# Sliding-window attention and MLP on one core: the transpose of x ahead of the turns by DMA, and k turned one block after q

## The chip, the core and the metric

The kernel runs on one core of one Trainium2 chip. The metric is the device time of one execution in microseconds. The engines are named as the profile names them: PE (TensorE, matmuls), DVE (VectorE), ACT (ScalarE), POOL (GpSimd), SP (SyncE, which here only issues DMAs). PEld is the load of weights into PE.

## The reference

For 8 batches, 8 heads, 576 positions and a head size of 64, attention with a window of 128 keys and a linear bias by distance, and then an MLP with a residual on the joined heads:

```python
scores = scale * np.matmul(q, k.transpose(0, 1, 3, 2))
bias = slopes[:, None, None] * (-np.abs(rel).astype(np.float32))[None, :, :]
mask = (rel >= 0) & (rel < window)
scores = np.where(mask, scores + bias[None], -1000000000.0)
attn = softmax(scores)                      # over the keys
x = (attn @ v), heads joined                # 8 x 576 x 512
xn = (x - mu) / np.sqrt(var + 1e-06) * g_ln
out = x + np.maximum(xn @ w_ch1, 0.0) @ w_ch2    # 512 -> 2048 -> 512
```

## The kernel before

**Blocks.** Two batches form a pair p (0 to 3). Each pair has nine blocks: blocks 0 to 7 are 128 positions of one of the two batches (block `2 i + b` is stretch i of batch b), and block 8, called T, holds the last 64 positions of both. In all there are 36 blocks, numbered n = 9 p + blk. The q and k of two neighbouring blocks (a pair of blocks, index i) are loaded, turned and kept together; the two halves of such a tile are transposed by separate instructions.

**Attention of a block.** `scores` (line 459, matmuls at L436) multiplies the turned q and k into PSUM, with the keys of the block itself and of the block two before it (the same batch, 128 positions back). For block T its call uses the keys of blocks 6 and 7 alone; T's own keys are used by `scores_tail` one block later. ACT takes the exponential (L445), DVE multiplies by the decay of the distance (`masks`, L456), `values` multiplies by v on PE (L489), and DVE divides by the sum (L497, L498) to give x.

**Normalisation.** `stats` takes mean and variance on DVE (L586, L587) and the inverse root on POOL (L541, L544, tile `rstd`). `normal` (line 524) centres and scales on DVE (L528, tile `xc`) and has SP transpose the result by DMA (L536) into `xT`, the MLP's input. Blocks 0 to 7 go another way, with a transpose on PE.

**MLP.** The blocks are gathered in groups: six of two blocks and then six of four (groups 0 to 5 and 6 to 11). `mlp1(g)` is 16 units of matmuls (L735) on all of a group's xT, so it can start when the last block of its group has been transposed. `mlp2` (L768) is the second product for the groups of two. Groups of four use `fast_mlp2` (L834), which multiplies with sums of quarters of w2 and of the hidden layer. The eight DVE instructions that build the sums of w2 (`combine_w2`, L189) are spread over earlier layers.

**q and k.** From pair (1, 2) on, that is from block 13, q and k are loaded by POOL's queue (L234) in a layout that a DMA can transpose, and SP transposes them into the turned tiles (L322, in `turn`): two transposes for q and two for k, one of each for block T. Before that, PE transposes them.

**Order.** The order is written out by hand. `steps` is a list of steps for the attention; for each block n from 8 on it holds

- values(n) and then the scores of block n + 2,
- masks(n + 1), masks(n + 2), stats(n) and the loads up to block n + 8 (`load_until`, on POOL),
- `turn_at(n + 1)`, which turns q and k of a pair that begins at block n + 5 where DMA does it,
- `normal(n)`, with xT(n).

Block 11 is `HURRIED`: normal(10) is put off to stand behind values(11) and the scores of block 13, so that blocks 10 and 11 follow each other with little MLP work between them. `weave_at` mixes the steps with the units of the MLP, unit by unit, by lists of places; `also` lists the units after which one instruction of the sums of w2 is put. Each engine runs its instructions in this order, and SP and POOL issue their DMAs in it. A store waits in SP's queue until its rows have been finished.

Of the kernel before, what the change touches and what calls it, by code (L numbers as in the profile page):

```python
# [22 lines left out]
T = 8  # L23
# [36 lines left out]
def kernel(  # L60
# [10 lines left out]
    nc = tc.nc  # L71
# [136 lines left out]
    raw = {}  # L208

    def by_dma(p, i):  # L210
        return (p, i) >= BY_DMA_TURN
# [41 lines left out]
    order = [(p, blk) for p in range(NPAIR) for blk in range(NSLOT)]  # L253
# [1 line left out]
    weights = {3: w1s + w2s[:2], 5: w2s[2:]}  # L255
    loads, place = [], []
    for n, (p, blk) in enumerate(order):
        if blk % 2 == 0:
            for src, tag in ((q, "q"), (k, "k")):
                loads.append((load_qk, src, tag, p, blk // 2))  # L260
        loads.append((load_v, p, blk))
        place.append(len(loads))
        loads += weights.get(n, [])
# [12 lines left out]
    turned = {}  # L276
# [30 lines left out]
    def turn(p, i, in_sc=False, copies=(nc.vector.tensor_copy, nc.scalar.copy)):  # L307

        k = keys_tile("k", p, i)
        q = queries(p, i) if i < 4 else keys_tile("q", p, i)
        if by_dma(p, i):
            for tag, dst in (("q", q), ("k", k)):
                src = raw.pop((tag, p, i))
                for b in range(2 if i < 4 else 1):
                    t = dst[:, b]
                    if tag == "q" and i < 4:  # L320
                        t = turned["q", p, i][:, b].rearrange("p h r c -> p h (r c)")
                    nc.sync.dma_start_transpose(  # L322
                        out=t, in_=src[:, b].rearrange("p h d -> p (h d)")
                    )
            return
        ps = [bank(b if in_sc else None) for b in range(2)]
        if i < 4:
            transposed("q", p, i, [t[:, 0] for t in ps])
            if p == 0 and i == 1:
                warm(3)  # L330
            transposed("k", p, i, [t[:, 1] for t in ps])
            for b, copy in enumerate(copies):
                copy(out=q[:, b], in_=ps[b][:, 0])
                copy(out=k[:, b].rearrange("p h (c r) -> p r h c", r=2), in_=ps[b][:, 1])
        else:
            for tag, t, dst, copy in zip("qk", ps, (q, k), copies):
                transposed(tag, p, i, [t[:, 0]])
                copy(out=dst[:, 0].rearrange("p h (c r) -> p r h c", r=2), in_=t[:, 0])

    def bank(sc=None):  # L340
        if sc is None:
# [6 lines left out]
    def queries(p, i):  # L348
        if by_dma(p, i):
            t = turned_pool.tile([P, 2, HP, 2, HALF], FP16, tag="q", name="q")  # L350
            turned["q", p, i] = t
            return t
        t = turned_pool.tile([P, 2, 2, HP, HALF], FP16, tag="q", name="q")
        turned["q", p, i] = t.rearrange("p b r h c -> p b h r c")
        return t

    def keys_tile(tag, p, i):
        t = turned_pool.tile([P, 2, HP, P], FP16, tag=tag, name=tag)
        turned[tag, p, i] = t
        return t  # L360
# [259 lines left out]
    for g, size in enumerate(GROUPS):  # L620
        n = sum(GROUPS[:g])
# [3 lines left out]
    count = len(order)  # L625

    def turn_step(n, *how):
        p, blk = order[n]
        return [(turn, p, blk // 2) + how]
# [28 lines left out]
    steps = warm_step(11) + [[(turn_first,)]] + warm_step(3)  # L658
# [7 lines left out]
    first = len(steps)  # L666
# [16 lines left out]
    steps += [[(scores_tail, 0)] + scores_step(9) + masks_of(8)]  # L683


    def turn_at(n):
        ahead = [m for m in (n + 3, n + 4) if m < count and order[m][1] % 2 == 0]
        return [
            f
            for m in ahead  # L690
            if by_dma(order[m][0], order[m][1] // 2) == (m == n + 4)
            for f in turn_step(m, True)
        ]

    steps.append(turn_at(8))
    for n in range(8, count):
        first_half, second_half = values_steps(n)
        step = first_half + second_half[:1]
        if n + 1 < count and order[n + 1][1] == T:
            step += [(scores_tail, order[n][0])]  # L700
        if n + 2 < count:
            step += scores_step(n + 2)
        steps.append(step)
        to_mask = [m for t in (n + 1, n + 2) if t < count for m in masks_of(t)]
        stats_step = [(stats, n)] + load_step(n)
        turns = [turn_at(n + 1)] if n + 1 < count else []
        if n == HURRIED:
            steps += [[(normal, n - 1)], to_mask + stats_step, [(normal, n)], *turns]
        else:
            steps += [to_mask + stats_step, *turns]  # L710
            if n != HURRIED - 1:
                steps.append([(normal, n)])
    combined = combine_w2()
    done = 0

# [10 lines left out]
    def mlp1(g, on_dve=()):  # L726
        xT = turned_x[g]
        w = w1 if g < FIRST_GROUPS else w1g
        cols = len(members[g]) * P
        ht = hidden[g] = hidden_pool.tile([P, NFB, 4 * P], FP16, tag="ht", name="ht")  # L730
        turn_about = chain(*zip(range(QF), range(QF, NFB)))
        for u, fb in enumerate(turn_about if g >= FAST else range(NFB)):
            ps = psum("ps_m1")
            for kb in range(NKB):
                nc.tensor.matmul(  # L735
                    ps[:, 0:cols],
                    w[:, kb, fb * P : (fb + 1) * P],
                    xT[:, kb, 0:cols],
                    start=(kb == 0),
                    stop=(kb == NKB - 1),  # L740
                )
            if u in on_dve:
                nc.vector.tensor_scalar(
                    out=ht[:, fb, 0:cols],
                    in0=ps[:, 0:cols],
                    scalar1=0.0,
                    scalar2=None,
                    op0=ALU.max,
                )
            else:  # L750
                nc.scalar.activation(  # L751
                    out=ht[:, fb, 0:cols], in_=ps[:, 0:cols], func=AF.Relu
                )
            yield cols
            if g >= FAST and u == 10:
                for i in range(4):
                    combine_hidden(g, 0, i)

    def mlp2(g, parts=((0, NFB),)):

        ht = hidden[g]
        sums = {}
        for first, end in parts:
            for at, (p, blk) in enumerate(members[g]):
                if first == 0:
                    sums[at] = ps_mm.tile([P, DM], FP32, tag="mm", name="ps_m2")
                for fb in range(first, end):
                    nc.tensor.matmul(  # L768
                        sums[at],
                        ht[:, fb, at * P : (at + 1) * P],  # L770
                        w2[:, fb, :],
                        start=(fb == 0),
                        stop=(fb == NFB - 1),
                    )
                    if fb % 4 == 3 and fb < NFB - 1:
                        yield DM
                if end == NFB:
                    finish(p, blk, sums[at])
                    yield DM
# [155 lines left out]
    def weave_at(units, *places, also=()):  # L935
        for u, _ in enumerate(units):
            advance_to(done + places.count(u))
            if u in also:
                next(combined, None)
# [13 lines left out]
    with tc.manual_schedule(engines={engine.PE, engine.SP, engine.Pool}):  # L953
        with tc.manual_schedule(engines={engine.Activation, engine.DVE}):
            advance_to(first)
            weave_at(mlp1(0, (0, 1)), 2, 7, 8, 9, 13)
            weave_at(mlp1(1), 2, 8, 12)
            weave_at(mlp2(0, ((0, 8), (8, 12), (12, NFB))), 0, 1, 3, 4, 4, 5)
            weave_at(mlp2(1), 0, 1, 2, 3, 4, 6, 6)
            weave_at(mlp1(2), 0, 3, 3, 6, 8, 11)  # L960
            weave_at(mlp2(2), 0, 2, 4, 6, 7)


            weave_at(mlp1(3, (9, 10, 11)), 8, 8, 12, 15)
            weave_at(mlp2(3), 0, 1, 1, 3, 4, 4, 6, 6)
            weave_at(mlp1(4), 0, 4, 8, 10, 10, 14)
            weave_at(mlp2(4), 0, 2, 2, 5, 5, 7, also=(1, 4, 6))
            weave_at(mlp1(5), 0, 5, 5, 8, 10, 12, also=(3, 6, 9))
            weave_at(mlp2(5), 0, 1, 2, 4, 6, 7)
            ring += [ps_mm.tile([P, DM], FP32, tag="mm", name="ps_r") for _ in range(4)]  # L970
            for g in range(6, len(GROUPS)):
                weave_at(
                    mlp1(g), 0, 2, 5, 7, 8, 10, 13, 15, also=(1, 4) if g == 6 else ()
                )
                weave_at(fast_mlp2(g), 1, 3, 6, 7, 7, 10, 12, 13)
# [31 lines left out]
```

## Time and profile before

| | |
|---|---|
| median of three runs | 315.26 us (314.24 to 315.96) |
| profiled execution | 315.53 us, span 313.8 us |
| mean granted clock of TensorE | 0.987 |
| PE busy | 300.4 us, 96% of the span |
| DVE busy | 220.6 us, 70% |
| ACT busy | 171.7 us, 55% |
| POOL busy | 140.0 us, 45% |
| transposes on SP | xT 28, q 23, k 23; median to landing 4.9, 5.8 and 5.0 us |

The profile is of one execution. Times in it are in us from the start of its span. A row of a timeline has its start, its length, the engine and line, the operation with its output and input, how many instructions were merged, and in brackets the idle time before it with what ended it. "SPq" is SP's issue of a DMA: its length is the time of the issue, and the landing comes later. A share of busy time says little by itself; what matters is which wait ends last where PE stands still.

### The profile page before, as it was taken

How to read it: one execution, taken by the hardware profiler on the slowest of the kernel's cores; microseconds unless marked ns; L12 is line 12 of the kernel's file. 1: busy time of each engine (PE TensorE's matmuls, PEld its weight loads, DVE VectorE, ACT ScalarE, POOL GpSimd, SP SyncE). 2: the span in 40 equal slices, each digit the busy share in tenths (PEclk: the TensorE clock that was granted, in tenths of full speed). 3: DMA queues.
4: the chain of work that ended last, by engine and by line, in shares of the span. 5: the costliest groups of instructions: out<-in, count | busy, mean ns of one | idle time of the engine just before them, and what ended most of it. 6: DMA issues, size and time to landing. Idle time of an engine off the chain costs nothing.

```text
span 313.8 us, 9068 instructions
## 1 busy us (share of the span) xinstructions
PE 300.4 (96%) x3747; PEld 200.8 (64%) x3747; DVE 220.6 (70%) x533; ACT 171.7 (55%) x297; POOL 140.0 (45%) x210
## 2 busy tenths in 40 slices
PE   8989999999999999699999999999999999999994
PEld 2468655757758575334885588558755874685484
DVE  2788877878585787806895799569948995761363
ACT  6587764767658376138427833772487247405600
POOL 8923756781287847822494618553301001100001
PEclk9999999999999999969999999999999999999999
DMA  9999999999799999990999999999945043015004
GB/s 112 164 204 200 185 155 162 198 108 141 94 96 156 159 170 170 145 204 18 105 120 188 144 87 99 174 177 97 138 95 118 19 88 85 18 28 125 0 2 134
DMA packets 150843, 38.28 MB, mean 122 GB/s; under 512 B 141809, under 2 KB 146417, under 8 KB 150802
## 3 DMA queue, kind: packets, MB, share of 16 engines
q0 software_dynamic: 103808, 18.49, 83.6%
q1 hardware_dynamic: 46594, 18.76, 35.7%
q8 instruction: 29, 0.48, 0.7%
q10 hardware_dynamic: 400, 0.46, 0.5%
q14 instruction: 12, 0.10, 0.1%
HBM read 36.90 MB, written 9.44 MB: 148 GB/s over the span
## 4 chain that ended last, share of the span: by engine, by line
PE 73%; POOL 8%; DVE 8%; DMA 6%; issue 2%; ACT 1%; POOLq 0%; DVEq 0%
PE ps_r L735 28%; PE ps_r L834 23%; PE ps_m L768 7%; PE ps_m L735 6%; DMA w<-in_moe_w_ch_dram 4%; PE ps_sc L436 4%; PE ps_r L489 3%; DMA xT<-xc 2%; DVE probs L456 2%; POOL vx L247 2%; POOL q L234 1%; DVE x L498 1%; POOL rstd L544 1%; DVE st L586 1%; POOL k L234 1%
## 5 line engine op out<-in xcount | busy, mean ns | idle before, releaser
L735 PEld LDWEIGHTS <-w1g 128*128 128x128 f16 x640 | 61.3, 99 | 55.9 <-issue 4.8
L735 PE MATMUL ps_r<-xT,w1g 128*128 128x512 f16 x384 | 87.6, 389 | 3.1 <-DMA xT<-xc 3.1
L445 ACT ACTIVATE probs<-ps_sc 128x1024 f16<-128x1024 f32 x56 | 54.2, 1026 | 56.0 <-PE ps_sc L436 56.0
L751 ACT ACTIVATE ht<-ps_r 128x512 f16<-128x512 f32 x96 | 56.1, 600 | 38.0 <-PE ps_r L735 38.0
L541 POOL TENSOR_TENSOR rstd<-moments,powers 128x1 f32<-128x1 f32 x28 | 8.0, 286 | 111.9 <-DVE moments L587 111.7
L768 PE MATMUL ps_m<-w,ht 128*128 128x512 f16 x192 | 45.5, 380 | 0.0
L834 PE MATMUL ps_r<-w,ht 128*128 128x256 f16 x384 | 43.9, 273 | 0.0
L456 DVE TENSOR_TENSOR probs<-probs,m 128x1024 f16<-128x1024 f16 x56 | 37.4, 688 | 6.5 <-ACT probs L445 6.2
L834 PEld LDWEIGHTS <-ht 128*128 128x128 f16 x384 | 37.2, 98 | 4.7
L751 ACT ACTIVATE ht<-ps_m 128x256 f16<-128x256 f32 x91 | 33.6, 387 | 9.3 <-PE ps_m L735 6.2
L247 POOL DMA_DIRECT2D vx<-in_v_dram x40 | 34.9, 882 | 7.2 <-DVE probs L456 2.1
L234 POOL DMA_DIRECT2D q<-in_q_dram x46 | 32.4, 714 | 0.7 <-DMA vx<-in_v_dram 0.5
L735 PE MATMUL ps_m<-xT,w1g 128*128 128x256 f16 x256 | 30.8, 273 | 2.0 <-DVE x L498 1.2
L768 PEld LDWEIGHTS <-ht 128*128 128x128 f16 x192 | 17.3, 98 | 18.0
L586 DVE BATCH_NORM_STATS2 st<-x 128x6 f32<-128x512 f16 x36 | 24.6, 684 | 0.0
L497 DVE RECIPROCAL rec<-ps_r 128x4 f32<-128x4 f32 x36 | 6.3, 175 | 25.3 <-PE ps_r L489 25.3
L234 POOL DMA_DIRECT2D k<-in_k_dram x26 | 22.2, 871 | 0.2
L834 PE MATMUL ps_r<-w,hs 128*128 128x256 f16 x192 | 21.9, 273 | 0.0
L489 PEld LDWEIGHTS <-probs 128*128 128x128 f16 x448 | 18.7, 97 | 4.7 <-DVE probs L456 0.3
L436 PE MATMUL ps_sc<-q,k 64*64 64x128 f16 (+1 forms) x1088 | 19.9, 208 | 1.6 <-ACT probs L445 1.0
L528 DVE TENSOR_SCALAR xc<-x,moments,rstd 128x512 f16<-128x512 f16 x28 | 11.9, 426 | 12.6 <-POOL rstd L544 10.7
L834 PEld LDWEIGHTS <-hs 128*128 128x128 f16 x192 | 18.8, 98 | 2.2
(87 smaller groups left out, 363.0 us busy)
## 6 DMA issues: line engine op xcount, KB each, us to landing
out_dram<-o SPq DMA_DIRECT2D x66, 128.0 KB, 3.5
k<-in_k_dram POOLq DMA_DIRECT2D x32, 128.0 KB, 6.1
vx<-in_v_dram POOLq DMA_DIRECT2D x32, 128.0 KB, 6.7
w<-in_moe_w_ch_dram POOLq DMA_DIRECT2D x8, 512.0 KB, 9.9
q<-in_q_dram POOLq DMA_DIRECT2D x48, 64.0 KB, 4.7
q<-in_q_dram POOLq DMA_DIRECT2D x12, 128.0 KB, 9.0
k<-in_k_dram POOLq DMA_DIRECT2D x8, 64.0 KB, 4.9
vx<-in_v_dram POOLq DMA_DIRECT2D x8, 64.0 KB, 4.7
```

The lines of the kernel that those rows point to most:

```text
L234: nc.gpsimd.dma_start(out=dst, in_=part.rearrange("h p d -> p h d"))
L247: nc.gpsimd.dma_start(out=vx[p0 : p0 + n, :, 0:D], in_=v[b, :, t0 : t0 + n, :].rearrange("h p d -> p h d"),)
L436: nc.tensor.matmul(in_halves(ps[cols, j, n, t, :])[:, r, queries], kt[rows, hp, cols], in_halves(qt[rows, b, hp])[:, r, queries], start=Tr ...
L445: nc.scalar.activation(out=dst.rearrange("p (n j) q -> p j n q", j=2), in_=ps.rearrange("p j n t q -> p j n (t q)"), func=AF.Exp, scale=in ...
L456: nc.vector.tensor_tensor(out=dst, in0=dst, in1=mask, op=ALU.mult)
L489: nc.tensor.matmul(ps[:, i, :], pr[:, h, t, :], vext[(p * NSLOT + o) % NV][:, h, :], start=(n == 0), stop=(n == len(terms) - 1),)
L528: nc.vector.tensor_scalar(out=xc, in0=xs[order[n]], scalar1=moments[:, n, 0:1], scalar2=rstd[:, n : n + 1], op0=ALU.subtract, op1=ALU.mult,)
L586: nc.vector.bn_stats(out=st, in_=xs[order[n]])
L735: nc.tensor.matmul(ps[:, 0:cols], w[:, kb, fb * P : (fb + 1) * P], xT[:, kb, 0:cols], start=(kb == 0), stop=(kb == NKB - 1),)
L751: nc.scalar.activation(out=ht[:, fb, 0:cols], in_=ps[:, 0:cols], func=AF.Relu)
L768: nc.tensor.matmul(sums[at], ht[:, fb, at * P : (at + 1) * P], w2[:, fb, :], start=(fb == 0), stop=(fb == NFB - 1),)
L834: nc.tensor.matmul(banks[name][pair][:, pair, :], lhs[:, fb, pair * P : (pair + 1) * P], rhs[:, fb, :], start=(first and fb == 0 and (pair ...
```

## The change

It has four parts. First, in every step SP issues the transpose xT(n) before any q or k transposes that belong to the same place. Second, where SP turns q and k, the turn is split in two: q of a pair beginning at block m is turned right behind normal(m - 5), about where both were turned before, and k right behind normal(m - 4), one block later. Third, the loads of k of such pairs (block T left out) are issued one block later than those of q, with the v of the second block. Fourth, two instructions of the sums of w2 move from the second layer of group 4, `mlp2(4)`, into its first layer, `mlp1(4)`.

```diff
     for n, (p, blk) in enumerate(order):
-        if blk % 2 == 0:
-            for src, tag in ((q, "q"), (k, "k")):
+        for src, tag in ((q, "q"), (k, "k")):
+            first = 1 if tag == "k" and blk < T and by_dma(p, blk // 2) else 0
+            if blk % 2 == first:
                 loads.append((load_qk, src, tag, p, blk // 2))
         loads.append((load_v, p, blk))
...
+    def turn_by_dma(tag, p, i):
+
+        if tag == "q" and i < 4:
+            queries(p, i)
+            dst = turned["q", p, i].rearrange("p b h r c -> p b h (r c)")
+        else:
+            dst = keys_tile(tag, p, i)
+        src = raw.pop((tag, p, i))
+        for b in range(2 if i < 4 else 1):
+            nc.sync.dma_start_transpose(
+                out=dst[:, b], in_=src[:, b].rearrange("p h d -> p (h d)")
+            )
...
+    def turned_by_dma(n):
+        return n < count and order[n][1] % 2 == 0 and by_dma(order[n][0], order[n][1] // 2)
+
     def turn_at(n):
-        ahead = [m for m in (n + 3, n + 4) if m < count and order[m][1] % 2 == 0]
-        return [
-            f
-            for m in ahead
-            if by_dma(order[m][0], order[m][1] // 2) == (m == n + 4)
-            for f in turn_step(m, True)
+        m = n + 3
+        if m >= count or order[m][1] % 2 or turned_by_dma(m):
+            return []
+        return turn_step(m, True)
+
+    def normal_step(n):
+
+        return [(normal, n)] + [
+            (turn_by_dma, tag, order[m][0], order[m][1] // 2)
+            for tag, m in (("q", n + 5), ("k", n + 4))
+            if turned_by_dma(m)
         ]
...
         if n == HURRIED:
-            steps += [[(normal, n - 1)], to_mask + stats_step, [(normal, n)], *turns]
+            steps += [normal_step(n - 1), to_mask + stats_step, normal_step(n), *turns]
         else:
             steps += [to_mask + stats_step, *turns]
             if n != HURRIED - 1:
-                steps.append([(normal, n)])
+                steps.append(normal_step(n))
...
-            weave_at(mlp1(4), 0, 4, 8, 10, 10, 14)
-            weave_at(mlp2(4), 0, 2, 2, 5, 5, 7, also=(1, 4, 6))
+            weave_at(mlp1(4), 0, 4, 8, 10, 10, 14, also=(2, 12))
+            weave_at(mlp2(4), 0, 2, 2, 5, 5, 7, also=(1,))
```

The branch of `turn` that turned q and k together by DMA goes.

More of the change, by code (lines that the diff above doesn't have):

```diff
@@ L314, in turn @@
         q = queries(p, i) if i < 4 else keys_tile("q", p, i)
[L315 to L325, printed above, removed]
         ps = [bank(b if in_sc else None) for b in range(2)]
```

## The prediction

> **What bounds the kernel now.** I number the 36 blocks n = 9p + blk, so xT(n) is the transposed input of block n, scores(n) its score matmuls, and k(13) stands for the keys of the pair 13/14, whose two transposes are k(13) first and second.
>
> I read the page first. PE is busy 96% of the span and the granted clock is full but for one place. The waits by engine show one long PE wait:
>
> ```profile
> DVE xc L528 <- POOL rstd L544: 10.7, 10, 3.2
> ...
> PE ps_r L735 <- DMA xT<-xc: 3.1, 1, 3.1
> ...
> PE ps_m L735 <- DVE x L498: 1.2, 3, 0.8
> ```
>
> Each line has the waiter, what it waited for, the total in us, how often, and the longest. The second is the start of the first group of four, mlp1(6), which needs xT(12) to xT(15). The stages around it, columns as headed:
>
> ```profile
> core 0: us, PE busy (x) PEld busy (x) DVE busy (x) ACT busy (x) POOL busy (x), PEclk, DMA share, GB/s
> 123.00:129.70 6.70, 6.70 (x96) 3.56 (x84) 5.38 (x14) 1.94 (x2) 3.60 (x7) 1.00 2.10 149
> 129.70:132.84 3.14, 0.01 (x3) 0.01 (x1) 2.71 (x8) 1.02 (x1) 3.14 (x4) 0.84 2.90 112
> 132.84:135.00 2.16, 2.16 (x6) 0.78 (x7) 1.08 (x3) 0.24 (x1) 2.08 (x4) 0.50 1.96 218
> 135.00:137.00 2.00, 2.00 (x6) 0.69 (x5) 0.00 (x0) 0.89 (x2) 0.12 (x1) 0.50 2.09 213
> 137.00:139.00 2.00, 2.00 (x7) 0.77 (x6) 0.00 (x0) 0.66 (x2) 0.00 (x0) 0.59 1.72 203
> 139.00:142.80 3.80, 3.80 (x25) 1.80 (x24) 0.00 (x0) 2.39 (x4) 0.00 (x0) 1.00 1.15 151
> ```
>
> PE stands still for 3.13 us and then runs at half clock for some 6 us. The chain that ended last prices this: the first 32 matmuls of mlp1(6) take 9.93 us, the next 32 take 7.02. So this place costs 3.13 + 2.91 us. SP's own queue shows why xT(15) is late:
>
> ```profile
> 121.52 2.66 SPq L322 DMA_TRANSPOSE q<-q  x2
> 124.28 2.52 SPq L322 DMA_TRANSPOSE k<-k  x2
> 126.90 1.22 SPq L536 DMA_TRANSPOSE xT<-xc  x1
> ```
>
> DVE had xc(15) ready at 123.25; SP was in the four transposes of pair 20/21 until 126.80, and xT(15) landed 5.9 us after its issue. After 132.84 PE waits for nothing until the end, so only the time before that can move the result. Between 83 and 130 PE has four more gaps: 0.77 at 93.28 (put down to DVE, but it fits xT(9): issued at 88.35, landed 4.8 later), and 0.19, 0.78 and 0.26 for banks that a late DVE has yet to read.
>
> **The change, part by part.** The counts stay: 28 xT, 23 q and 23 k transposes at about 1.25 us of SP each, the same stores and loads. Only order moves.
>
> *xT ahead.* xT(n) no longer stands behind up to four transposes (5 us). For xT(15) in the clock of before: it can issue at about 121.5 (below) instead of 126.90, and lands about 127, where PE gets to mlp1(6) at about 130. I take the 3.13 and the 2.91 as gone; cover is 3 us.
>
> *The w2 sums.* Two of eight 0.68 us DVE instructions move from 109.41 and 110.87, where they stand in front of xc(13) and values(14), to units 2 and 12 of mlp1(4), where DVE waits for rstd (3.17 us idle before xc(11)). They hide there; without that cover they cost 1.4 us of DVE, not of PE.
>
> *k loaded a block later.* On POOL a block's q, k and v loads (2.85 + 1.80 + 0.93 us) stand in front of the next rstd. rstd(11) started at 98.42, with its moments ready at 96.17; without the two k issues it starts 1.8 us sooner, which is what DVE waited for. The k loads then stand behind rstd of the odd blocks with v (2.7 us), 5 us or more before the next rstd, and land some three blocks ahead of their use. No cost. With DVE back in time I take the gaps of 0.19, 0.78 and 0.26 as gone too; if they stay, add 1.2.
>
> *k turned a block later.* This is the cost. k of the pair beginning at m now stands on SP behind xT(m-4), thus behind DVE's xc(m-4), and scores(m) come at step m-2 on PE, which takes nothing out of turn. Queued behind it on PE is everything, MLP matmuls included. Where blocks are 8 us of PE or more apart, as after 133 (scores every 7.5 us, and two steps between), this is covered: k(22) would issue near 152 and scores(22) came at 165.05. Before 133 it is not always. The order there squeezes blocks 10 and 11 together:
>
> ```profile
> 87.34 0.54 PE L436 MATMUL ps_sc<-q,k 64*64 64x128 f16 x32
> 87.82 2.76 PE L768 MATMUL ps_m<-w,ht 128*128 128x512 f16 x12
> 90.42 0.65 PE L489 MATMUL ps_pv<-vx,probs 128*128 128x65 f16 x16
> 90.99 0.54 PE L436 MATMUL ps_sc<-q,k 64*64 64x128 f16 x32
> ```
>
> The last line is scores(13). SP had this around it:
>
> ```profile
> 88.35 1.92 SPq L536 DMA_TRANSPOSE xT<-xc  x1
> 90.35 1.18 SPq L931 DMA_DIRECT2D out_dram<-o  x2
> ```
>
> The 88.35 is xT(9), issued as soon as xc(9) was there (88.32), and nothing upstream of xc(9) gets earlier: scores(11) at 83.01, two exponentials to 85.42, masks, statistics, rstd to 87.87. So k(13) first issues at about 90.3. It has no row of its own there; the bounds are 3.6 us to landing (its own transposes in before, in light traffic) and 5.6 (q(15) at 91.70), and the nearest is xT(9) with 4.8, in the same loads. That is 95.1, against 91.0: PE idles 4.1 us (2.2 if the issue takes 1.22 and the landing 3.6; 4.9 with 5.6). The 0.77 at mlp1(4) falls into it.
>
> An idle of 4.1 is longer than the 3.13 that cost 2.91 of half clock, so I charge 2.91 again; the bounds are 0 (the 0.78 gap shows no loss) and 2.91. [...]
>
> The other places: k(15) issues near 103.5 in the shifted clock and lands 5.3 to 7.6 later, scores(15) come near 110.3: nothing to 0.8 us, I take nothing. k(17) is needed only by the tail scores at step 16: covered by 2 us. k(18) stands behind xT(13), q(18) twice, k(17), two stores and xT(14). xc(13) can be there at 110.3 (5.3 us after scores(15) at 104.96); the queue adds 1.2 + 2.6 + 1.2 + 1.2, with 0.5 between them, and xT(14) 1.25: k(18) issues near 118.2 and lands near 123.3 (rows of before: k(18) 4.1, q(18) 6.1, I take 5.1). scores(18) would be due at 123.05 less the 1.04 of gaps saved, 122.0. Idle 1.2 us (0.3 to 2.3), too short for the clock. xT(15) is behind both k(18) transposes, done at 120.8, and xc(15) comes near 121: it issues at once.
>
> **The sum**, against the profiled execution (315.53, span 313.8; 1.7 us lie around the span and stay). Gone: 3.13 + 2.91 + 0.77 + 0.19 + 0.78 + 0.26 = 8.04. New: 4.1 + 2.91 + 1.2 = 8.21. Net +0.2, 315.7; the median of the three runs is 0.27 lower than the profiled one, so 315.4. A measurement here can tell about 0.5%, 1.6 us, from no change.
>
> **Rivals.**
> *The new wait stays short (faster).* If k(13) lands by 94.1, PE idles less than the 3.1 that is known to drop the clock. With 3.6 to landing and a 1.22 issue: 2.2 + 0.3 - 8.04 = -5.5, 309.8; just under the point: 3.1 + 1.2 - 8.04 = -3.7, 311.5. For it: k(13)'s own 3.6, xT(8)'s 2.5. Against: those fell into light traffic, while POOL issues six loads from 87.83 on.
> *A second clock fall at scores(18) (slower).* Everything in that queue is serial; from an idle of 3.1 on (k(18) landing 7 us after issue) the clock goes again: 4.1 + 2.91 + 3.1 + 2.91 - 8.04 = +5.0, 320.2. For it: xT(10) and xT(11) took 7.5 and 7.6 to land. Against: the rows from 110.8 to 120.1 lie between 4.1 and 6.1.
> *The purpose fails: xT(15) still late (slower).* If DVE is later than I have it and eats the 3 us of cover, the 6.04 stays: 8.21 - 2.00 = +6.2, 321.5. For it: the chain from 83 to 127 runs through DVE and POOL, not PE. Against: PE's own new delay of 4 to 7 us gives DVE time.
>
> **How the numbers follow.** Forecast 0.48, short wait 0.29, second fall 0.17, xT(15) late 0.06. The forecast alone spans 313.4 (half clock and wait each 1.0 less) to 317.3 (wait 4.9, scores(18) 2.3): of its 0.48, 0.09 lies below 313.7, 0.32 within 0.5%, 0.07 above. So faster 0.38, same 0.32, slower 0.30. The range 310.9 to 319.6 leaves out the lowest part of the short wait (0.07) and most of the two slow cases (0.13).
>
> **What would show it.** Right: a PE wait on a k transpose at L436 near 91 to 95, a clock of 0.50 after it, no wait at the first matmul on ps_r, and full clock there; rstd(11) right behind its moments; xT(9), k, k in this order on SP. Wrong: no PE gap near 91 (then k landed sooner than any row here), or gaps above 3 us at scores(15) or scores(18), or waits after the first four-block group, where I expect none.

## The result: 3.4% slower

The changed kernel takes 326.94 us (median of six runs, 323.6 to 329.45) against 315.08 before. The ratio of the means, without the one slow run of 329.45 us, is 1.0344, with a 95% interval of 1.028 to 1.0408. The profiled execution took 326.98 us, its span is 325.2. The prediction was 315.4 with a range of 310.9 to 319.6.

The waits by engine, in the changed kernel (its line numbers: 439 are the scores, 746 is the first MLP layer, 779 the second of the groups of two, 539 xT, 339 the turns by DMA):

```profile
PE ps_sc L439 <- DMA k<-k: 13.3, 6, 5.1
...
DVE xc L531 <- POOL rstd L547: 7.7, 10, 0.9
...
PE ps_m L746 <- ACT ht L762: 0.6, 2, 0.3
```

The wait for xT(15), 3.1 us, is gone, and so are the gaps that the prediction put down to a late DVE. In their place PE waits six times for a k transpose, 13.3 us in all. DVE's longest wait for rstd fell from 3.2 to 0.9 us. PE's timeline at the first wait:

```profile
91.37 0.25 PE L439 MATMUL ps_sc<-q,k 64*64 64x128 f16 x4
96.69 0.80 PE L439 MATMUL ps_sc<-q,k 64*64 64x128 f16 x28 [5.07 <-DMA k<-k]
97.42 1.89 PE L779 MATMUL ps_m<-w,ht 128*128 128x512 f16 x4
99.11 6.63 PE L746 MATMUL ps_m<-xT,w1g 128*128 128x256 f16 x44
```

These are the scores of block 13: four matmuls with the old keys, then 5.07 us in which PE stands still. The four matmuls behind it take 1.89 us instead of 1.04, the next 44 take 6.63 instead of 4.96. SP's queue at the time, and the granted clock (the column PEclk) by the microsecond:

```profile
88.73 1.76 SPq L539 DMA_TRANSPOSE xT<-xc  x1
90.65 2.52 SPq L339 DMA_TRANSPOSE k<-k  x2
```

```profile
core 0: us, PE busy (x) PEld busy (x) DVE busy (x) ACT busy (x) POOL busy (x), PEclk, DMA share, GB/s
94.00:95.00 1.00, 0.00 (x0) 0.00 (x0) 0.00 (x0) 0.00 (x0) 1.00 (x3) 1.00 2.48 114
95.00:96.00 1.00, 0.00 (x0) 0.00 (x0) 0.00 (x0) 0.00 (x0) 1.00 (x2) 0.83 1.61 102
96.00:97.00 1.00, 0.31 (x16) 0.31 (x20) 0.00 (x0) 0.00 (x0) 1.00 (x2) 0.50 1.50 225
...
102.00:103.00 1.00, 1.00 (x9) 0.78 (x8) 0.70 (x2) 0.58 (x2) 0.71 (x2) 0.75 0.70 191
103.00:104.00 1.00, 1.00 (x12) 0.90 (x10) 0.41 (x1) 0.87 (x3) 1.00 (x2) 1.00 0.00 0
```

k(13) issued right behind xT(9), at 90.65, and landed 6.0 us later. The clock is at half from about 95.7 to 102.5; 5.8 us of that lie behind the restart at 96.69, and half of them, 2.9 us, is the loss. The same happens at the scores of block 18, and three shorter waits follow in the second half of the kernel:

```profile
129.89 0.32 PE L439 MATMUL ps_sc<-q,k 64*64 64x64 f16 x16
133.50 0.64 PE L439 MATMUL ps_sc<-q,k 64*64 64x128 f16 x16 [3.29 <-DMA k<-k]
134.07 6.60 PE L779 MATMUL ps_m<-w,ht 128*128 128x512 f16 x24
...
181.22 0.51 PE L439 MATMUL ps_sc<-q,k 64*64 64x128 f16 x28 [1.96 <-DMA k<-k]
...
204.66 0.41 PE L439 MATMUL ps_sc<-q,k 64*64 64x128 f16 x16 [0.93 <-DMA k<-k]
...
236.66 0.51 PE L439 MATMUL ps_sc<-q,k 64*64 64x128 f16 x28 [1.92 <-DMA k<-k]
```

The wait for k(18) costs 3.29 us and, at half clock until 136.6, 1.55 more. The last three are scores(24), (27) and (31); scores(15) waited 0.16. The account of the profiled executions: waits for k 5.07 + 0.16 + 3.29 + 1.96 + 0.93 + 1.92 = 13.33, half clock 2.9 + 1.55 = 4.45, two new waits for ACT 0.58; gone are the 8.04 of before. That is +10.3 of the measured +11.45. Of the 1.1 us left, 0.4 lie ahead of 83 us (scores(11) start at 83.39 and not 83.01). The rest is not shown by a row of its own; an estimate is that each wait costs some 0.2 us more than the idle time that the profile shows. From the start of scores(15) to the next product it is 0.84 us in the change and 0.48 before, for a wait of 0.16; the six waits for k come to 1.2 us by this, and the waits that went give part of it back.

### The profile page after: what moved, and what is told of

The parts are those of the page before. It is cut to its first block, busy times and chain, and to the rows that moved or that the text cites. A ratio compares the mean times of both kernels' runs of the same rounds, so it can differ in the third digit from the quotient of the medians.

```text
span 325.2 us, 9067 instructions
## 1 busy us (share of the span) xinstructions
PE 303.0 (93%) x3747; PEld 202.9 (62%) x3747; DVE 221.9 (68%) x533; ACT 171.8 (53%) x297; POOL 140.7 (43%) x210
## 4 chain that ended last, share of the span: by engine, by line
PE 71%; DMA 17%; DVE 4%; POOL 3%; ACT 2%; issue 1%; SPq 0%; DVEq 0%; POOLq 0%
PE ps_r L746 24%; PE ps_r L845 19%; DMA k<-k 12%; PE ps_m L779 10%; PE ps_m L746 8%; PE ps_sc L439 4%; DMA w<-in_moe_w_ch_dram 4%; ACT probs L448 2%; PE ps_r L492 2%; PE ps_pv L492 1%; POOL vx L247 1%; DVE probs L459 1%; POOL k L237 1%; POOL q L237 1%; PE ps_sc L302 1%
## 5 line engine op out<-in xcount | busy, mean ns | idle before, releaser
L746 PE MATMUL ps_r<-xT,w1g 128*128 128x512 f16 x384 | 84.8, 379 | 0.0
L779 PE MATMUL ps_m<-w,ht 128*128 128x512 f16 x192 | 47.6, 393 | 0.0
L439 PE MATMUL ps_sc<-q,k 64*64 64x128 f16 (+1 forms) x1088 | 21.6, 211 | 14.8 <-DMA k<-k 13.3
L746 PE MATMUL ps_m<-xT,w1g 128*128 128x256 f16 x256 | 32.2, 282 | 0.7 <-ACT ht L762 0.6
L439 PEld LDWEIGHTS <-k 64*64 64x64 f16 x1088 | 15.4, 109 | 20.5 <-DMA k<-k 14.1
L448 ACT ACTIVATE own<-ps_sc 128x1024 f16<-128x1024 f32 x12 | 12.1, 1032 | 18.1 <-PE ps_sc L439 17.6
```

The source lines that it names most:

```text
L439: nc.tensor.matmul(in_halves(ps[cols, j, n, t, :])[:, r, queries], kt[rows, hp, cols], in_halves(qt[rows, b, hp])[:, r, queries], start=Tr ...
L448: nc.scalar.activation(out=dst.rearrange("p (n j) q -> p j n q", j=2), in_=ps.rearrange("p j n t q -> p j n (t q)"), func=AF.Exp, scale=in ...
L746: nc.tensor.matmul(ps[:, 0:cols], w[:, kb, fb * P : (fb + 1) * P], xT[:, kb, 0:cols], start=(kb == 0), stop=(kb == NKB - 1),)
L779: nc.tensor.matmul(sums[at], ht[:, fb, at * P : (at + 1) * P], w2[:, fb, :], start=(fb == 0), stop=(fb == NFB - 1),)
```

## The experiments

Theory A: the loss is k's turn behind xT(m-4), which ties it to DVE's xc(m-4) and leaves too little time before scores(m), and all else in the change gains. Theory B: the transposes crowd each other or the moved loads hurt, and order only hands the delay on. Times below are medians; the kernel before had 315.14, 315.37 and 314.95 us in the three sets (e1 to e4, e5 to e8, e9 to e11).

**e1: k beside q.** The changed kernel with

```diff
-            for tag, m in (("q", n + 5), ("k", n + 4))
+            for tag, m in (("q", n + 5), ("k", n + 5))
```

> The changed kernel with one part undone: k is turned in the same place as q, behind xT(m-5), not a block later behind xT(m-4). Theory A (the loss is k's turn standing behind xT(m-4), and so behind DVE's xc(m-4)): the six waits of PE for a k transpose (13.3 us) and the 4.4 us of half clock that follow two of them go, while the wait for xT(15), its half clock and the small gaps of before (8.0 us) stay away: 307 to 309 us, median 308. Theory B (the loss comes from the transposes landing later whatever their order, because xT, q and k crowd SP's queue or the loads moved): PE still waits for k, and the time stays above 315.

314.34 us, ratio 0.9971 (0.9951 to 0.999). The waits for k shrink to one of 0.61 us, as A has it, and the loss of the change goes; but the gain that A counted on is not there. SP's queue and PE in this run:

```profile
84.09 2.17 SPq L539 DMA_TRANSPOSE xT<-xc  x1
86.44 2.52 SPq L339 DMA_TRANSPOSE q<-q  x2
89.12 3.57 SPq L339 DMA_TRANSPOSE k<-k  x2
92.80 1.22 SPq L539 DMA_TRANSPOSE xT<-xc  x1
```

```profile
98.60 6.24 PE L746 MATMUL ps_m<-xT,w1g 128*128 128x256 f16 x44 [3.59 <-DMA xT<-xc]
```

Four transposes that no longer stand ahead of xT(8) stand ahead of xT(9) instead. xc(9) was ready at 90.0, its transpose issued at 92.80, and mlp1(4) waited 3.59 us; its first 44 matmuls then took 6.24 us, at a granted clock of 0.61 from 98.6 to 102.0, where they took 4.96 before. Here B is right: "xT first" in a step puts the turns right ahead of the next xT.

**e2: turns first, k still a block late.** The changed kernel with `normal_step` returning the q and k transposes and then `(normal, n)`.

> The changed kernel with the q and k transposes of a step issued ahead of its xT again, k still one block behind q. Theory A (k is late because it waits in SP's queue for xc(m-4)): k(13) can issue near 85, the wait at 91 goes; k(18) stands behind xT(13) only and its wait shrinks below 1 us; xT(15) has two transposes in front and not four (2.7 us instead of 5.3), so it lands at about the time PE needs it: 307 to 312 us. Theory B (one block later is too late in itself): the waits for k of 5.1 and 3.3 us stay within 1 us of that, 322 or more.

313.33 us, ratio 0.9961 (0.993 to 0.9993). k(13) issues at 83.98, ahead of xT(9), and its wait is gone; at this place one block later is thus not too late in itself, against B. At scores(18) and scores(24) k is late even so, by 1.69 and 1.28 us, and xT(15) by 0.74; with these A's number was missed by 1.3 us.

```profile
124.00 0.41 PE L439 MATMUL ps_sc<-q,k 64*64 64x128 f16 x16 [1.69 <-DMA k<-k]
131.51 7.07 PE L746 MATMUL ps_r<-xT,w1g 128*128 128x512 f16 x32 [0.74 <-DMA xT<-xc]
170.36 0.51 PE L439 MATMUL ps_sc<-q,k 64*64 64x128 f16 x28 [1.28 <-DMA k<-k]
```

**e3: only xT first.** The kernel before with xT(n) ahead of the q and k of its step, nothing else.

> The kernel before with one part of the change alone: xT(n) is issued ahead of the q and k of the same step; k turned with q, loads and w2 sums as before. Theory A: the wait for xT(15) of 3.1 us and its 2.9 us of half clock go, the small gaps for a late DVE (2.0 us) stay: 308 to 310 us. Theory B (the queue order is not what made xT(15) late; DVE and POOL were): 313 or more.

311.27 us, ratio 0.9895 (0.9861 to 0.9928). mlp1(6) starts without a wait: the queue order was what made xT(15) late. A expected 308 to 310. At mlp1(4) the profiled execution waits longer than the 0.77 us of before, as in e1, and loses clock behind it (0.61 from 96 to 98):

```profile
96.00 6.63 PE L745 MATMUL ps_m<-xT,w1g 128*128 128x256 f16 x44 [1.89 <-DMA xT<-xc]
```

This execution took 313.73 us. It is one of four of the ten that took 312.4 to 313.9 us at a mean granted clock of 0.989 to 0.994; the other six took 309.9 to 311.3 at 0.998 to 1.0. So the loss of clock behind this wait is not in the median.

**e4: matmuls in the gap of the kernel before.** One line, `warm(14)`, ahead of mlp1(6): 14 matmuls whose result nobody uses.

> The kernel before with 14 idle matmuls of 128x512 (3.0 us at full clock) put in the 3.1 us gap ahead of mlp1(6); nothing else. If the 2.9 us of slow matmuls behind the gap are the half clock that follows an idle PE, they go and the gap stays: 312 to 313 us, the first 32 matmuls of mlp1(6) in 7.0 to 7.3 us. If they have another cause (xT's bank, the transfers): no change, 315.

312.52 us, ratio 0.9909 (0.9882 to 0.9936), 2.6 us less:

```profile
129.26 3.19 PE L283 MATMUL ps_warm<-ones 128*128 128x512 f16 x14
132.66 7.08 PE L735 MATMUL ps_r<-xT,w1g 128*128 128x512 f16 x32 [0.20 <-DMA xT<-xc]
```

xT(15) lands no sooner, but the 32 matmuls take 7.08 us where they took 9.93. The 2.9 us were the clock. Three of the 48 executions of the kernel before that ran beside the experiments agree: at a mean clock of 0.997 to 1.0, without idle matmuls, they took 312.3 to 312.8 us.

**e5: q and k together, the first pair early.** The changed kernel with k beside q as in e1, and for the pair 13/14 alone both turned ahead of xT(8), where SP is idle:

```diff
+        return turns + [(normal, n)] if n == 8 else [(normal, n)] + turns
```

> Loads and w2 sums as in the change, every xT ahead of the turns of its step and k turned with q behind xT(m-5), but for the first pair: q(13) and k(13) are turned ahead of xT(8), where SP is idle, as in the kernel before. Theory A (the late k is all of the loss; xT(9) of the run with k beside q was late only because q(13) and k(13) stood behind xT(8) and so right ahead of xT(9)): no PE wait above 1 us after 70 us, full clock there, all 8.0 us of before gained: 307 to 309 us. Theory B (moving the queue only hands the delay on to another transpose): a wait of 2 us or more for another xT or k, 311 or more.

308.40 us, ratio 0.9789 (0.9757 to 0.9821): 2.1% faster than the kernel before. The mean granted clock of the profiled execution is 0.998, and these are the largest waits of PE:

```profile
PE ps_warm L284 <- DVE vx L956: 1.5, 1, 1.5
PE ps_sc L439 <- ACT probs L448: 1.1, 2, 0.6
PE ps_m L747 <- ACT ht L763: 0.6, 2, 0.3
PE ps_m L747 <- DMA xT<-xc: 0.5, 1, 0.5
```

The first two stand at the start, the others are short.

**e6: e5 with the loads and the sums of w2 as before.**

> As the run with q(13) and k(13) ahead of xT(8), with the loads of k and the w2 sums back where the kernel before has them. Theory A: the small gaps of a late DVE (0.78, 0.26, 0.19) return and nothing else: 1 to 2 us slower than that run, 308 to 311. If the loads or the sums cost by themselves, this run is the faster of the two.

310.15 us, ratio 0.9838 (0.9818 to 0.9858), 1.75 us more than e5 in the same set. The gaps for DVE return (0.39, 0.58 and 0.26 us, 1.23 in all, as much as the prediction had counted), and there is a wait of 0.38 us for k at scores(15). Loads and sums together are worth a little more than the prediction took for those gaps.

**e7: e5 with k a block late from the pair 20/21 on.**

> As the run with q(13) and k(13) ahead of xT(8), but from the pair 20/21 on k is turned a block later, as in the change. Theory A as the trace of the change shows it: the waits for k(24), k(27) and the second half of k(31)'s pair of 2.0, 0.9 and 1.9 us are there, none falls the clock: 4 to 5 us more than that run, 312 to 313. What the prediction had: a late k is covered after the first group of four: no difference, below 309.

312.45 us, ratio 0.9925 (0.9892 to 0.9959), 4.05 us more than e5. Waits for k stand at scores(20), (27) and (31), 0.45, 0.44 and 1.32 us in the profiled execution (311.94 us); mlp1(4) waited 1.32 us for xT(9) in it too, against 0.51 in e5, although nothing that the edit moves stands ahead of that. The waits are smaller and not all at the same blocks as in the change. That a late k is covered in the second half is refuted by these waits and by the time; where all of the 4 us lie, one profile does not show.

**e8: matmuls inside the two long waits.** The changed kernel with `warm(20)` ahead of scores(13) and `warm(11)` ahead of scores(18).

> The changed kernel with 20 idle matmuls of 128x512 (4.3 us) ahead of scores(13) and 11 (2.4 us) ahead of scores(18), inside the two long waits for k; nothing else. If half clock after an idle PE is what stretches the matmuls behind those waits (2.9 and 1.55 us), both go and the waits stay: 322 to 323 us. If not, no change: 327.

318.50 us, ratio 1.0099 (1.0076 to 1.0122), below the 322 to 323 expected. The mean granted clock is 1.0 and the matmuls behind the first wait are back at their old length:

```profile
91.78 4.48 PE L284 MATMUL ps_warm<-ones 128*128 128x512 f16 x20
96.19 0.25 PE L439 MATMUL ps_sc<-q,k 64*64 64x128 f16 x4
96.95 0.51 PE L439 MATMUL ps_sc<-q,k 64*64 64x128 f16 x28 [0.51 <-DMA k<-k]
97.39 1.04 PE L779 MATMUL ps_m<-w,ht 128*128 128x512 f16 x4
98.27 4.97 PE L746 MATMUL ps_m<-xT,w1g 128*128 128x256 f16 x44
```

The gain of 8.4 us is more than the 4.45 of clock. In the second half the profiled execution waited 1.45 us for k, against 4.81 in the changed kernel's; why those shrank is open.

**e9: k a block late up to the pair 18/19 only.** The changed kernel with k beside q from 20/21 on.

> The changed kernel with k turned beside q from the pair 20/21 on, so that only k(13) to k(18) are a block late. If the parts add up: the 308.4 us of the run with q(13) and k(13) early, plus the waits for k(13) and k(18) (5.1 and 3.3 us) and their half clock (2.9 and 1.6): 320 to 323 us; no wait for k after 150 us. If the waits of the second half feed on the first (a late k(18) makes k(24) late): waits for k stay there, 325 or more.

320.95 us, ratio 1.0193 (1.0143 to 1.0243). The parts nearly add up: e5, plus 4.05 for the second half (e7) and 12.55 for the first (this run less e5), gives 325.0, where the change has 326.9 with a spread of 6. The 12.55 is the price of the first half as the change has it: e9 differs from e5 in the place of q(13) as well as in the late k. The waits:

```profile
95.32 0.80 PE L439 MATMUL ps_sc<-q,k 64*64 64x128 f16 x28 [4.38 <-DMA k<-k]
...
127.99 0.32 PE L439 MATMUL ps_sc<-q,k 64*64 64x64 f16 x16 [0.42 <-DMA k<-k]
133.53 0.64 PE L439 MATMUL ps_sc<-q,k 64*64 64x128 f16 x16 [5.22 <-DMA k<-k]
```

No wait for k comes after 150 us. scores(18) waited 5.22 us for k here and 3.29 in the change: the landing took 6.8 us here and 5.9 there, and k(18) was issued 1.6 us before PE stopped here and 2.7 there.

**e10 and e11: the loads or the sums alone.** e5 with the loads of before, and e5 with the sums of before.

> The run with q(13) and k(13) early, with the loads of k back beside those of q; w2 sums as in the change. If the loads are what brings DVE back in time (rstd(11) behind two k issues on POOL): most of the 1.75 us that loads and sums were worth together goes, 309.5 to 310. If the sums are: 308.4 to 308.8.

> The run with q(13) and k(13) early, with the two w2 sums back in mlp2(4); loads as in the change. If the sums are what DVE was late by: 309.5 to 310, with the wait of about 0.6 us for o at the second unit of mlp1(5) back. If the loads are: 308.4 to 308.8.

309.33 us, ratio 0.9824 (0.9783 to 0.9865), and 309.43, ratio 0.9843 (0.9791 to 0.9895). Each lies about 1 us above e5, which was measured in another set; their intervals overlap those of both e5 and e6, so how the 1.75 us divide is not settled. The traces show each at its own place: without the moved loads PE waits 0.58 us for DVE at mlp1(4), behind rstd(11), whose POOL instructions start at 97.72 behind two k loads and at 96.42 without them in e5; without the moved sums a wait of 0.58 us for o at the second unit of mlp1(5) is back, which stood at 0.78 in the kernel before.

## Why the prediction was wrong

**The step that failed: "where blocks are 8 us of PE or more apart, as after 133 ..., this is covered".** It compared k(22), issued near 152, with scores at 165.05 and called those scores(22). Counting the rows of scores from 129.29, which is scores(19), 165.05 is scores(23); scores(22) came at 158.75. The slack was overstated by a block, 6.3 us, and one pair stood for all; nor does the condition of 8 us fit the 7.5 us between scores that the same sentence names. k(22) itself is in time in the change. k(24), behind four stores and xT(20), issued at 173.98 and landed 7.2 us later, while scores(24) were due near 179.3. From the issue to the need it is 5.3 us there, 5.4 for k(27) and 5.2 for k(31), which landed after 6.3 and 7.0. The sum had nothing for this, and waits after the first group of four were what the prediction had named as a sign of being wrong. The changed kernel's trace shows 4.81 us of waits, and e7, which adds the late k of the second half to e5, is 4.05 us slower than e5. Of the 11.3 us between the forecast and the profiled execution this is the largest part; k(18) has 3.6 and k(13) 1.0.

**k(18): the term of the sum that was mis-sized.** The sum had 1.2 us and no loss of clock. Measured: 3.29 and 1.55. The queue was read rightly, but each link was a little longer: k(18) issued 15.0 us after the start of scores(15) and not 13.2, and took 5.9 and not 5.1 to land. That the wait passes into a second fall of the clock was the rival "A second clock fall at scores(18)", given 0.17, with 3.1 us as its point; the wait passed it by 0.2. That an idle time of up to 2.3 us is too short for the clock was the author's estimate: the rows of before show no loss behind 0.78 us and one behind 3.13, and e3 lost clock behind 1.89.

**k(13): right in place, short in size.** 4.1 us predicted, 5.07 measured. The issues held: xT(9) at 88.73 and k at 90.65, against 88.35 and 90.3 predicted. The landing took 6.0 us, outside the bounds of 3.6 to 5.6, which had been taken from only three rows.

**The clock behind it: right, and its size by luck.** 2.91 us charged, 2.9 measured; e4 and e8 show that it is the clock. But the loss depends on when the fall comes: behind the same wait, 4.38 us long in e9 (granted clock 0.50 from 95.3 to 98, 0.77 from 98 to 102), half clock ended 4.5 us after the restart, and not 5.8, and cost 2.2.

**What is gained: right, and the change hid it.** Of 8.04 us counted, e5 has 7.0 in the medians. The loads and the sums do what the prediction said (1.75 us together against 1.2 of gaps), and xT(15) comes in time. "xT first" alone, though, does not give the 6.0 us: e3 has 3.9, and its trace shows why in part: the turns that leave the front of xT(8) stand ahead of xT(9).

With the three terms as measured (k(13) and k(18) with their clock 12.55 by e9, the second half 4.05 by e7, against the 7.0 that e5 gains) the sum would have been +9.6 us.

## What to carry to other kernels

When a DMA is moved behind another one in a queue, its earliest issue becomes that one's release (k(13) issued at 90.65 behind xT(9) in the change, at 83.98 ahead of it in e2); write out for every consumer the time from that release to its need, block by block, and check the numbering of the rows against a form that occurs only once. When the slack of an engine that sets the end comes out near zero, price it with the worst landing in the trace and not the nearest. A better order need not delay anything: e5 keeps the two gains and puts the first pair where the queue is idle.

## What the runs showed of the hardware

A DMA transpose of 128x512 fp16 within SBUF occupies SP for 1.2 to 1.3 us in most rows (median of the 28 of xT in the change 1.22), and the time from its issue to its landing varies widely: 2.4 us for q(13) in e1, 7.6 for k(15) and 8.4 for xT(20) in the changed kernel. k(13) took 2.7 us in e2 and 6.0 in the change. No run isolates what makes the difference.

The length of an idle time alone does not decide whether PE's clock falls. In the traces it fell with the wait of 1.89 us in e3 and with the waits of 3.13 us in the kernel before, 3.29 and 5.07 in the change, 3.59 in e1, and 4.38 and 5.22 in e9, none of them filled by idle matmuls. It stayed at 1.00 with the waits of 1.96 and 1.92 us in the changed kernel and with 1.69 in e2. The rows of e3:

```profile
94.10:96.00 1.90, 0.01 (x2) 0.03 (x2) 1.87 (x6) 0.86 (x1) 1.90 (x3) 1.00 1.82 211
96.00:98.00 2.00, 2.00 (x12) 1.51 (x13) 1.75 (x4) 0.77 (x2) 2.00 (x4) 0.61 1.61 151
98.00:100.00 2.00, 2.00 (x12) 1.43 (x11) 0.00 (x0) 0.77 (x2) 2.00 (x3) 0.54 1.98 152
```

With half clock at 0.50, these shares put the fall near 96.4, 0.4 us behind the restart, and the full clock near 99.8, a loss of 1.7 us.

The falls came at different distances from the start of the wait: in the kernel before at 131.81, 2.1 us into it; in the change at 95.67, 4.0 us into the wait for k(13), and at 133.21, 3.0 us into that for k(18). Half clock lasted 6.83 us in the kernel before and at scores(13) of the change, and 3.41 at scores(18) of the change, 30.72 us behind the end of the stretch at scores(13); by the granted clock it was some 3.4 us in e1 and e3, and some 6.9 twice in e9. What a fall cost lay between 1.55 us, at scores(18) of the change, and 2.9, in the kernel before and at scores(13) of the change. So a wait of 1.89 us cost clock here and one of 1.96 did not; no run isolates what decides it.
